# Reordering the start of a delta-rule and SwiGLU kernel: norms first, zero fills on another engine, two units alone in the first chain, filler products, and a written order that ends early

## The chip, the cores and the metric

The kernel runs on one core of one Trainium2 chip. The metric is the device time of a run in microseconds (us); the time before is the median of three runs. The profile is one execution of the same program, taken by the hardware profiler. Its engines are TensorE (PE; its weight loads are listed apart as PEld), VectorE (DVE), ScalarE (ACT), GpSimd (POOL) and SyncE (SP), which in the kernel before issues every DMA.

## The reference

Two blocks follow each other. The first is a delta-rule recurrence over 768 tokens, for 4 batches and 8 heads of width 48. Its output, seen as 3072 tokens of width 384, goes through an RMS norm and a SwiGLU feed-forward layer (FFN) of inner width 1536. All is float32; the four weight tensors are handed over as float64, and the kernel before reads them as pairs of 32-bit words and makes float32 of them on the chip.

```python
k_n = k / (np.linalg.norm(k, axis=-1, keepdims=True) + 1e-06)
for t in range(S):
    kt, vt, bt = (k_n[:, :, t], v[:, :, t], beta[:, :, t, None])
    y[:, :, t] = np.einsum('bhd,bhde->bhe', q[:, :, t], state)
    v_old = np.einsum('bhde,bhd->bhe', state, kt)
    state = state + bt[:, :, :, None] * np.einsum('bhd,bhe->bhde', kt, vt - v_old)
# ... x = y as (3072, 384)
xn = x / np.sqrt(np.mean(x * x, axis=-1, keepdims=True) + 1e-06) * rms_g
g = xn @ w_gate
out = (g * (1.0 / (1.0 + np.exp(-g))) * (xn @ w_val)) @ w_out
```

## The kernel before

Tokens are taken in chunks of 128, so there are 6 chunks of 4 units (one batch each). For each unit the keys are normalised, keys and queries are transposed (`kqt`), and their products (`gp`) are taken. Within a chunk the recurrence becomes a triangular system. Its 32x32 diagonal blocks, of all heads and batches at once, are gathered through DRAM (`gd`, `gblk`) and inverted by VectorE in 31 steps (`invert`). The inverses go back through DRAM (`td` to `tt`, and scaled `nd` to `ne`), and `recur` joins the blocks, solves, and updates the state. Every two units of output make one FFN group of 256 tokens.

Each part is a Python generator; `at(time, gen)` gives its place on a plan, and the plan's order is the written order of the program. Inside `manual_schedule` that order is kept on every engine. A plan unit is three FFN products and a little more: an FFN group takes 36.

```python
    def setup():
        # ... loads, constants, masks
        yield 3.5
        # ... beta transposed
        for t in [tt_all] + state:
            nc.gpsimd.memset(t, 0.0)
        nc.gpsimd.memset(gp_all[HC:C, :, 0:HC], 0.0)
        yield 6
        for n in range(B):
            load_v(n)
        load_k(B)

    def weights(times):                 # 18 pieces of 768 columns
        for (dst, src), raw, (time, dt) in zip(todo, raws, times):
            # ...
            nc.scalar.activation(out=top, in_=high.bitcast(FP32), func=ACTF.Copy, scale=2.0**-112)
            # ... five VectorE operations (L224 to L252), fetch() of a later piece before the last

    def normalize(n):
        kn = kpad[n % NK]
        nc.scalar.square(ksq, kn[:, :, 0:D])
        nc.vector.tensor_reduce(out=ksum, in_=ksq, axis=AXL.X, op=ALU.add)
        nc.vector.tensor_scalar_max(ksum, ksum, 1e-30)
        nc.gpsimd.tensor_tensor(out=knrm, in0=ksum, in1=half, op=ALU.pow)
        yield
        # ... + 1e-6, reciprocal, multiply

    def gather(n):                      # L337, L342
        for a in range(NBLK):
            nc.sync.dma_start(out=gds[c][...], in_=gp[b][...])
        if b == B - 1:
            nc.sync.dma_start(out=gblk, in_=gds.pop(c))

    def invert(c, dt):
        # ... ttb = identity
        for i in range(W - 1):          # 31 steps
            nc.vector.scalar_tensor_tensor(out=tmp, ...)        # L401
            nc.vector.tensor_tensor(out=to, in0=to, in1=tmp, op=ALU.add)   # L410
            yield dt
        nc.sync.dma_start(out=td, in_=ttb)
        nc.vector.tensor_tensor(out=gblk, in0=ttb..., in1=nbeta..., op=ALU.mult)
        nc.sync.dma_start(out=nd, in_=gblk)
        for b in range(B):
            # ... four tt loads from td (L426), two ne loads from nd (L431)

    def recur(c, dt):
        # corner: p_v, p_w -> vs, tt; inner: p_x, p_z -> x, u; outer: p_k, p_y, p_s -> v, y, state
        for s in range(-3, B + 2):
            inner(s, s - 1, s + 1)
            yield dt
            outer(s + 1, s - 1)
            yield dt
            corner(s + 3, s + 2)
            if s - 2 in units:
                transpose_y(B * c + s - 2, ys.pop(s - 2))
            yield dt

    def ffn(m, f0, f1):                 # FT = 12 feature blocks
        for f in range(f0, f1):
            # ... 6 products into p_gv (L645), sil on ScalarE (L654), h_f on VectorE (L656),
            # ... then the 2 products into p_o (L632) of the block before

    at(23, invert(0, 0.74))
    at(51.5, recur(0, 0.8))
    for i, m in enumerate((0, 1, 0, 1)):
        at(TF + CYC // 4 * i, ffn(m, half_f * (i // 2), half_f * (i // 2 + 1)))     # TF = 68, CYC = 72
    # ... weights: 3 pieces early, 5 from 47.5, 10 from TF + 1
    for c in range(1, NCH):
        t0 = TF - 16 + CYC * c
        for b in range(B):
            at(t0 - 57 + 5 * b, prepare(B * c + b))
        at(t0 - 30.5, invert(c, 0.55))
        at(t0 - 9, recur(c, 1.2))
        # ... two FFN groups at t0 + 16
    with tc.manual_schedule():
        run_plan()
```

Of the kernel before, what the change touches and what calls it, by code (L numbers as in the profile page):

```python
# [18 lines left out]
C = 128  # L19
# [8 lines left out]
def kernel(  # L28
# [74 lines left out]
    vraw = {}  # L103
# [30 lines left out]
    def setup():  # L134
# [25 lines left out]
        for i, p in enumerate((lo, hi)):  # L160
            nc.vector.tensor_tensor(
                out=mask[p, i], in0=row[p, p], in1=col[p, p], op=ALU.is_lt
            )
        yield 15
# [3 lines left out]
        yield 3.5  # L168
# [6 lines left out]
        for t in [tt_all] + state:  # L175
            nc.gpsimd.memset(t, 0.0)
        nc.gpsimd.memset(gp_all[HC:C, :, 0:HC], 0.0)
        yield 6
        for n in range(B):
            load_v(n)  # L180
        load_k(B)

# [28 lines left out]
    def weights(times):  # L211
        clock = 0
        for (dst, src), raw, (time, dt) in zip(todo, raws, times):
            yield time - clock
            clock = time + 5 * dt
            two = raw.bitcast(U32).rearrange("p (n two) -> p n two", two=2)
            low, high = two[:, :, 0], two[:, :, 1]
# [3 lines left out]
            top = bits.tile([128, WT], FP32, name="top", bufs=2)  # L221
            top_u, dst_u = top.bitcast(U32), dst.bitcast(U32)
            nc.scalar.activation(out=top, in_=high.bitcast(FP32), func=ACTF.Copy, scale=2.0**-112)
# [17 lines left out]
            yield dt  # L241

# [14 lines left out]
    def normalize(n):  # L257
# [4 lines left out]
        nc.vector.tensor_reduce(out=ksum, in_=ksq, axis=AXL.X, op=ALU.add)  # L262

        nc.vector.tensor_scalar_max(ksum, ksum, 1e-30)  # L264
        knrm = work.tile([128, H], FP32, name="knrm")
# [65 lines left out]
    def gather(n):  # L331
# [3 lines left out]
        for a in range(NBLK):  # L335
            o = diagonal(a)
            nc.sync.dma_start(  # L337
                out=gds[c][a * BH + b * H : a * BH + (b + 1) * H].rearrange("h r j -> r h j"),
                in_=gp[b][W * a : W * (a + 1), :, o : o + W],
            )  # L340
# [51 lines left out]
    def invert(c, dt):  # L392
# [3 lines left out]
        for i in range(W - 1):  # L396
# [13 lines left out]
            nc.vector.tensor_tensor(out=to, in0=to, in1=tmp, op=ALU.add)  # L410
            yield dt
        td = dram.tile([128, W, W], FP32, name="td")
# [9 lines left out]
        nc.sync.dma_start(out=nd, in_=gblk)  # L422
        for b in range(B):
            for a in (1, 3, 0, 2):
# [4 lines left out]
                )  # L429
            for a in (0, 2):  # L430
# [10 lines left out]
    def recur(c, dt):  # L441
# [35 lines left out]
        def outer(b_k, b_y):  # L477
# [11 lines left out]
            for h in range(H):  # L489
                for p, place in ((lo, Q0), (hi, Q1)):  # L490
# [7 lines left out]
                    )  # L498
            if c < NCH - 1:
# [10 lines left out]
                for par in range(2):  # L510
                    p = slice(DP * par, DP * (par + 1))
                    to = st[p, :, D * par : D * (par + 1)]
                    if c == 0:
                        nc.vector.tensor_copy(out=to, in_=p_s[p])
                    else:
                        nc.vector.tensor_tensor(out=to, in0=to, in1=p_s[p], op=ALU.add)
            if n + NK < NU:
                load_k(n + NK)
            if n + B < NU:
                load_v(n + B)  # L520
            ys[b_y] = norm(p_y)
# [59 lines left out]
        ys = {}  # L581
        for s in range(-3, B + 2):
# [4 lines left out]
            corner(s + 3, s + 2)  # L587
            if s - 2 in units:
# [3 lines left out]
    def norm(p_y):  # L592
# [10 lines left out]
        nc.vector.tensor_scalar_add(ms, ms, 1e-6)  # L603
        rs = work.tile([128, 1], FP32, name="rs")
        nc.gpsimd.tensor_tensor(out=rs, in0=ms, in1=mhalf, op=ALU.pow)  # L605
        nc.scalar.mul(y, p_y.rearrange("p h d -> p (h d)"), rs)
# [79 lines left out]
    def run_plan():  # L686
        heap = list(plan)
        heapq.heapify(heap)
        while heap:
# [9 lines left out]
    for n in range(B):  # L699

        times = (3.5 + 1.2 * n, 6.6 + 1.7 * n, 7.4 + 2.1 * n, 10.2 + 2.1 * n, 24 + 4 * n, 26 + 4 * n, 48 + 3 * n)
        at(0, prepare_first(n, [b - a for a, b in zip((0,) + times, times)]))
    at(23, invert(0, 0.74))
    at(51.5, recur(0, 0.8))
    half_f = FT // 2
    for i, m in enumerate((0, 1, 0, 1)):
# [4 lines left out]
            [(8.5 + 4.5 * i, 0.85) for i in range(3)]  # L711
            + [(47.5 + 4.2 * i, 0.8) for i in range(5)]
            + [(TF + 1 + 3.1 * i, 0.6) for i in range(10)]
        ),
    )
    for c in range(1, NCH):
        t0 = TF - 16 + CYC * c
        for b in range(B):
            at(t0 - 57 + 5 * b, prepare(B * c + b))
        at(t0 - 30.5, invert(c, 0.55))  # L720
        at(t0 - 9, recur(c, 1.2))
        for g in range(B // 2):
            at(t0 + 16 + CYC // 2 * g, ffn(B // 2 * c + g, 0, FT))
    with tc.manual_schedule():
        run_plan()
# [30 lines left out]
```

## Time and profile before

| what | before |
|---|---|
| time, median of 3 runs (lowest, highest) | 939.84 us (936.17, 942.12) |
| span of the profiled execution | 939.0 us |
| PE busy | 817.7 us (87%) |
| PEld busy | 628.8 us (67%) |
| DVE busy | 417.8 us (44%) |
| ACT busy | 247.4 us (26%) |
| POOL busy | 86.7 us (9%) |
| mean granted TensorE clock | 0.931 of full |

An engine's share is an average over stages that have different limits. The page also slices the run into 40 equal parts, with the busy share of each engine and the clock that TensorE was granted in tenths, and the trace can be asked for the busy time in any window and for what ended an engine's idle time. In the names, `out<-in` is what an instruction writes and reads, and L645 is line 645 of the kernel. A float32 product shows as two instructions in the trace. The first FFN product stands at 114.1 us, the four middle chunks take 140.7 to 142.1 us each, and the last stretch takes 100.6 us.

### The profile page before, as it was taken

The numbers are of one execution on the slowest core, as the hardware profiler recorded it, in microseconds if no ns is written. First come the engines' busy times: TensorE is split into PE (matmuls) and PEld (weight loads), VectorE is DVE, ScalarE is ACT, GpSimd is POOL, SyncE is SP. The second block draws the span as 40 slices with busy tenths as digits, with TensorE's granted clock in tenths as the row PEclk, the third lists the DMA queues.
The fourth block names the chain that finished last, engine by engine and source line by source line (L and its number), as shares of the span: only waits on it lengthen the run. The fifth ranks groups of instructions, "written<-read, shape, count | busy, mean of one in ns | idle before, by whom it ended". The sixth has DMA issues, their size and how long they took to land.

```text
span 939.0 us, 19558 instructions
## 1 busy us (share of the span) xinstructions
PE 817.7 (87%) x8270; PEld 628.8 (67%) x8270; DVE 417.8 (44%) x1053; ACT 247.4 (26%) x677; POOL 86.7 (9%) x94
## 2 busy tenths in 40 slices
PE   4516587879999979999979999979999979999998
PEld 3315465657777757777757777757777757777776
DVE  6796468893234292234283233283233283221010
ACT  4513234301314311324311324311324301221101
POOL 5000123000012100012100012100012100000000
PEclk8555689979999999999989999999999989999999
DMA  7724434303022103022203022203021103000000
GB/s 201 172 65 130 113 93 130 111 0 96 19 62 43 46 18 80 19 60 43 44 20 79 20 52 41 49 25 79 20 61 24 25 31 79 3 19 1 17 1 17
DMA packets 150935, 51.80 MB, mean 55 GB/s; under 512 B 142368, under 2 KB 145440, under 8 KB 150848
## 3 DMA queue, kind: packets, MB, share of 16 engines
q1 hardware_dynamic: 150848, 50.55, 22.0%
q8 instruction: 65, 1.06, 0.5%
q14 instruction: 22, 0.18, 0.1%
HBM read 36.37 MB, written 14.16 MB: 54 GB/s over the span
## 4 chain that ended last, share of the span: by engine, by line
PE 72%; DVE 12%; DMA 5%; ACT 5%; issue 3%; SPq 2%; POOL 1%; DVEq 0%; ACTq 0%; POOLq 0%
PE p_gv L645 36%; PE p_o L632 18%; DVE tmp L401 4%; DVE ttb L410 4%; PE p_y L491 3%; PE p_t L286 2%; PE p_g L302 2%; DMA gblk<-gd 2%; PE p_z L544 2%; PE p_k L526 2%; ACT gp L312 2%; ACT gp L311 2%; PE p_y L526 2%; DMA gd<-gp 1%; PE p_x L562 1%
## 5 line engine op out<-in xcount | busy, mean ns | idle before, releaser
L632 PE MATMUL p_o<-wo_sb,h_f 128*128 128x384 f32 x576 | 221.3, 509 | 42.3 <-DVE h_f L656 42.0
L645 PE MATMUL p_gv<-xt,wg_sb 128*128 128x256 f32 x864 | 222.3, 395 | 3.8 <-DVE xt L616 3.8
L645 PE MATMUL p_gv<-xt,wv_sb 128*128 128x256 f32 x864 | 215.3, 385 | 0.0
L645 PEld LDWEIGHTS p_gv<-xt,wg_sb 128*128 128x128 f32 x864 | 165.9, 197 | 48.5 <-DVE xt L616 4.2
L645 PEld LDWEIGHTS p_gv<-xt,wv_sb 128*128 128x128 f32 x864 | 162.8, 193 | 23.9 <-issue 1.4
L632 PEld LDWEIGHTS p_o<-wo_sb,h_f 128*128 128x128 f32 x576 | 106.0, 194 | 96.5 <-DVE h_f L656 51.3
L656 DVE TENSOR_TENSOR h_f<-sil,p_gv 128x256 f32<-128x256 f32 x144 | 60.2, 418 | 230.7 <-ACT sil L654 230.6
L654 ACT ACTIVATE sil<-p_gv 128x256 f32<-128x256 f32 x144 | 55.1, 383 | 241.4 <-PE p_gv L645 225.5
L401 DVE SCALAR_TENSOR_TENSOR tmp<-gblk,nbeta,ttb 128x31 f32<-128x31 f32 (+15 forms) x186 | 74.7, 402 | 33.3 <-DMA gblk<-gd 28.0
L605 POOL TENSOR_TENSOR rs<-ms,mhalf 128x1 f32<-128x1 f32 x24 | 15.0, 625 | 617.1 <-DVE ms L603 617.1
L410 DVE TENSOR_TENSOR ttb<-ttb,tmp 128x31 f32<-128x31 f32 (+15 forms) x186 | 63.7, 343 | 7.0 <-DVE tmp L401 0.3
L316 DVE TENSOR_TENSOR gp<-p_g,mask 64x128 f32<-64x128 f32 (+1 forms) x160 | 37.9, 278 | 51.6 <-ACT gp L312 47.0
L302 PE MATMUL p_g<-kqt 64*64 64x192 f32 (+2 forms) x896 | 46.3, 338 | 5.0 <-ACT kqt L291 4.0
L266 POOL TENSOR_TENSOR knrm<-ksum,half 128x8 f32<-128x8 f32 x24 | 40.6, 1696 | 105.7 <-DVE ksum L264 105.7
L291 ACT COPY kqt<-p_t 128x512 f32<-128x512 f32 x48 | 28.1, 586 | 70.1 <-PE p_t L286 69.8
L302 PEld LDWEIGHTS p_g<-kqt 64*64 64x64 f32 x896 | 34.8, 153 | 17.2 <-issue 8.4
L596 ACT ACTIVATE y<-p_y 128x384 f32<-128x384 f32 x24 | 11.8, 491 | 110.2 <-PE p_y L491 110.2
L562 PE MATMUL p_x<-tt,gp 64*64 64x64 f32 x384 | 30.7, 237 | 9.5 <-ACT tt L474 9.5
L311 ACT COPY gp<-p_g 128x128 f32<-128x128 f32 x96 | 25.6, 266 | 48.9 <-PE p_g L302 47.2
L472 ACT COPY vs<-p_v 32x256 f32<-32x256 f32 x48 | 17.4, 362 | 77.2 <-PE p_w L464 52.8
L457 PE MATMUL p_v<-tt,gp 32*32 32x32 f32 x768 | 19.6, 201 | 19.1 <-DMA tt<-td 19.1
L457 PEld LDWEIGHTS p_v<-tt,gp 32*32 32x32 f32 x768 | 16.7, 113 | 28.7 <-issue 26.5
(83 smaller groups left out, 757.6 us busy)
## 6 DMA issues: line engine op xcount, KB each, us to landing
kpad<-in_k_dram SPq DMA_DIRECT2D x24, 192.0 KB, 2.8
raw<-in_moe_w_gate_dram SPq DMA_DIRECT2D x6, 768.0 KB, 5.3
qpad<-in_q_dram SPq DMA_DIRECT2D x24, 192.0 KB, 3.3
raw<-in_moe_w_val_dram SPq DMA_DIRECT2D x6, 768.0 KB, 4.4
v_raw<-in_v_dram SPq DMA_DIRECT2D x24, 192.0 KB, 3.3
raw<-in_moe_w_out_dram SPq DMA_DIRECT2D x6, 768.0 KB, 4.6
out_dram<-o_sb SPq DMA_DIRECT2D x24, 192.0 KB, 1.9
gd<-gp SPq DMA_DIRECT2D x96, 32.0 KB, 1.7
```

Source lines behind the costliest of these rows:

```text
L266: nc.gpsimd.tensor_tensor(out=knrm, in0=ksum, in1=half, op=ALU.pow)
L302: nc.tensor.matmul(to, pair[d, K1 if i else K0], pair[d, places], skip_group_check=True)
L311: nc.scalar.copy(to[:, :, K0], p_g[:, :, K0])
L316: nc.vector.tensor_tensor(out=to[p, :, place], in0=p_g[p, :, place], in1=mask[p, i, None].to_broadcast([p.stop, 2, HC]), op=ALU.mult,)
L401: nc.vector.scalar_tensor_tensor(out=tmp, in0=gblk[:, i, None, i + 1 :].to_broadcast(shape), scalar=nbeta[:, c, i : i + 1], in1=ttb[:, 0 : ...
L410: nc.vector.tensor_tensor(out=to, in0=to, in1=tmp, op=ALU.add)
L526: nc.tensor.matmul(p_o[p, 2 * j : 2 * j + 2].rearrange("p h d -> p (h d)"), kq[:, j, place], st[:, j], start=(alone or j == 0), stop=alone ...
L562: nc.tensor.matmul(p_x[lo, h], gp[b_x][hi, h, HC * K0 : HC * (K0 + 1)], tt[b_x][hi, h], skip_group_check=True,)
L632: nc.tensor.matmul(p_o[i], h_f[:, i * C : (i + 1) * C], wo_sb[:, f], start=(f == f0), stop=(f == f1 - 1),)
L645: nc.tensor.matmul(p_gv[:, i], w_sb[:, t, f * 128 : (f + 1) * 128], xt[:, t], start=(t == 0), stop=(t == KT - 1),)
L654: nc.scalar.activation(out=sil, in_=p_gv[:, 0], func=ACTF.Silu)
L656: nc.vector.tensor_tensor(out=h_f, in0=sil, in1=p_gv[:, 1], op=ALU.mult)
```

## The change

The start is reordered, and some work goes to other engines.

- *Norms first.* All four units' norms stand ahead of the weight conversion on VectorE; the maximum goes to GpSimd, as does the addition in the RMS norm of the output. Two weight pieces instead of three come early, and each piece's first ScalarE step is written ahead, so that VectorE need not wait for it.
- *Zero fills* of `tt`, `gp` and the states go from GpSimd to ScalarE, spread between its copies.
- *Gathers* (`gd`) are issued by ScalarE, which wrote the data, and no longer by SyncE. `nd` is issued after the first unit's `tt` loads.
- *Two units alone.* In the first chunk, units 0 and 1 go through the recurrence by themselves, then units 2 and 3, so that the first FFN group can begin before units 2 and 3 are done. The state's update of the first chunk is a ScalarE copy, and it comes last.
- *Useless products.* TensorE multiplies the identity by itself, or by the inversion's intermediate, into a PSUM tile that nobody reads, to stay busy while it would wait.
- *Scale apart.* The norm's last multiplication is written a step after the norm, so that ScalarE does other work while GpSimd computes the factor.
- *Written order only up to half a cycle.* `manual_schedule` ends at plan time 104; what follows is ordered by the framework's own scheduler, and the plan's places for the later chunks are moved a little.

The diff, cut to its core:

```diff
+        p_fill.append(psum.tile([128, DM], FP32, name="p_fill", tag="out", bufs=2))
+        stay_warm(14)
...
-        for t in [tt_all] + state:
-            nc.gpsimd.memset(t, 0.0)
-        nc.gpsimd.memset(gp_all[HC:C, :, 0:HC], 0.0)
-        yield 6
+        yield 5
         for n in range(B):
             load_v(n)
         load_k(B)
+        yield 3
+        nc.scalar.memzero(tt_all)
+        yield 4
+        nc.scalar.memzero(gp_all[HC:C, :, 0:HC])
+        yield 4
+        for t in state:
+            nc.scalar.memzero(t)
+    def stay_warm(n, data=ident):
+        for i in range(n):
+            nc.tensor.matmul(
+                p_fill[0][:, 0 : data.shape[1]], ident, data, skip_group_check=True
+            )
...
-        nc.vector.tensor_scalar_max(ksum, ksum, 1e-30)
         knrm = work.tile([128, H], FP32, name="knrm")
+        nc.gpsimd.tensor_scalar_max(ksum, ksum, 1e-30)
...
-            nc.sync.dma_start(
+            nc.scalar.dma_start(
                 out=gds[c][a * BH + b * H : a * BH + (b + 1) * H].rearrange("h r j -> r h j"),
...
+            if c == 0 and i > W // 2:
+                stay_warm(2, tmp_b[:, 0 : min(128, n * (i + 1))])
             yield dt
+        if c == 0:
+            stay_warm(22)
...
-        nc.sync.dma_start(out=nd, in_=gblk)
         for b in range(B):
             # ... the four tt loads
+            if b == 0:
+                nc.sync.dma_start(out=nd, in_=gblk)
...
+            ys[b_y] = norm(p_y)
+            if c > 0:
+                update(b_y, u)
...
+        if c == 0:
+            for a, b in ((0, 1), (2, 3)):
+                corner(a, None)
+                stay_warm(warm)
+                yield dt
+                corner(b, a)
+                yield dt
+                # ... inner, corner, outer of a and b, with stay_warm(warm) between
+                transpose_y(a, scale(*ys.pop(a)))
+                stay_warm(warm)
+                yield dt
+                transpose_y(b, scale(*ys.pop(b)))
+                stay_warm(warm)
+                yield dt
+                update(a, u_a)
+                yield dt
+                update(b, u_b)
+                reload()
+                dt, warm = 1.2, 0
+                yield dt
+            return
...
-        nc.vector.tensor_scalar_add(ms, ms, 1e-6)
         rs = work.tile([128, 1], FP32, name="rs")
+        nc.gpsimd.tensor_scalar_add(ms, ms, 1e-6)
         nc.gpsimd.tensor_tensor(out=rs, in0=ms, in1=mhalf, op=ALU.pow)
+        return y, p_y, rs
+
+    def scale(y, p_y, rs):
         nc.scalar.mul(y, p_y.rearrange("p h d -> p (h d)"), rs)
...
-    at(23, invert(0, 0.74))
-    at(51.5, recur(0, 0.8))
+    at(20.9, invert(0, 0.74))
+    at(49, recur(0, 1.5, 3))
...
-            [(8.5 + 4.5 * i, 0.85) for i in range(3)]
-            + [(47.5 + 4.2 * i, 0.8) for i in range(5)]
-            + [(TF + 1 + 3.1 * i, 0.6) for i in range(10)]
+            [(12 + 4.2 * i, 0.8) for i in range(2)]
+            + [(46 + 4.2 * i, 0.8) for i in range(5)]
+            + [(TF + 1 + 3.1 * i, 0.6) for i in range(11)]
...
+        first = TF + 2 if c == 1 else t0 - 60
         for b in range(B):
-            at(t0 - 57 + 5 * b, prepare(B * c + b))
-        at(t0 - 30.5, invert(c, 0.55))
-        at(t0 - 9, recur(c, 1.2))
+            at(first + 4.5 * b, prepare(B * c + b))
+        at(first + 27, invert(c, 0.68))
+        at(*((t0 - 4, recur(c, 0.9)) if c == 1 else (t0 - 9, recur(c, 1.2))))
...
     with tc.manual_schedule():
-        run_plan()
+        run_plan(TF + CYC // 2)
+    run_plan()
```

In the program that results, each step's TensorE order is what the prediction counts from: after the change 120 FFN products stand ahead of the second chunk's recurrence, 102 before it; from the third chunk on both numbers are the same.

## The prediction

> **What bounds the kernel now.** I read four views: the page's slices for the course of the run, a table of windows cut at the kernel's own milestones, then the timeline in the two places where TensorE waits. A "unit" is one batch of one 128-token chunk; four units make a chunk, six chunks the run.
>
> From the page, busy tenths and granted clock in 40 slices of 23.5 us:
>
> ```profile
> PE   4516587879999979999979999979999979999998
> DVE  6796468893234292234283233283233283221010
> PEclk8555689979999999999989999999999989999999
> ```
>
> TensorE is full from the eighth slice on except one dent per chunk; the first five slices are half empty and at half clock; DVE is full just before each dent. The windows put numbers on it (start:end, length, then busy us of PE, weight loads, DVE, ACT, POOL, and the clock):
>
> ```profile
> 36.70:62.50 25.80, 6.20 (x72) 4.60 (x72) 23.09 (x62) 5.73 (x20) 0.00 (x0) 0.50 0.39 85
> 62.50:114.00 51.50, 26.57 (x646) 23.68 (x646) 33.50 (x54) 14.60 (x34) 3.44 (x4) 0.57 0.48 130
> 114.00:216.00 102.00, 83.75 (x477) 62.98 (x478) 81.90 (x182) 31.42 (x75) 14.49 (x11) 0.89 0.30 85
> 273.50:414.20 140.70, 131.89 (x1389) 100.95 (x1388) 58.32 (x164) 36.57 (x103) 12.93 (x15) 0.99 0.20 44
> 838.40:939.00 100.60, 97.15 (x455) 75.72 (x453) 11.76 (x28) 12.67 (x33) 0.54 (x1) 1.00 0.03 12
> ```
>
> First inversion (DVE alone), first recurrence (no engine full, clock 0.57), then from the first FFN product at 114 to the end of the second inversion at 216, where DVE converts weights, masks scores and inverts: 81.9 of 102. After that four chunks of about 141 us, TensorE-bound, and a tail. The dent in a chunk, from the timeline (start, length, engine, line, in brackets the idle time before and who ended it):
>
> ```profile
> 328.43 0.25 DVE L401 SCALAR_TENSOR_TENSOR tmp<-gblk,nbeta,ttb 128x31 f32<-128x31 f32 x1 [5.17 <-DMA gblk<-gd]
> 331.17 1.56 PE L632 MATMUL p_o<-wo_sb,h_f 128*128 128x384 f32 x4 [1.18 <-DVE h_f L656]
> 341.31 2.93 PE L632 MATMUL p_o<-wo_sb,h_f 128*128 128x384 f32 x4 [4.34 <-DVE h_f L656]
> ```
>
> DVE waits 5.17 for the gathered blocks with an h_f queued behind it, then runs 62 inversion operations with h_f spaced by up to 14 of them: TensorE loses 5.5 us, once per chunk. And the start:
>
> ```profile
> 11.76 3.27 DVE L224 TENSOR_SCALAR top<-top 128x768 uint32<-128x768 uint32 x1 [1.83 <-ACT top L223]
> 17.78 1.08 PE L286 MATMUL p_t<-ident,kpad 128*128 128x128 f32 x4 [4.78 <-DVE kpad L271]
> 84.61 0.89 ACT L223 ACTIVATE top<-raw 128x768 f32<-128x768 f32 x1 [4.31 <-DMA raw<-in_moe_w_out_dram]
> ```
>
> A weight operation that is 0.56 elsewhere takes 3.27 and delays unit 2's norm; at 84.6 ScalarE sits on a weight load for 4.31 with the recurrence's copies behind it.
>
> **What the Trainium skill says.** "SBUF — State Buffer", Who interferes with whom: a VectorE tensor_scalar in a two-port mode and GpSimd exclude each other for a whole instruction. The trace agrees: the 3.27 lies on GpSimd's zero fills (tt 1.80 from 11.38, state 1.50 from 13.12). "TensorE: Matmul & The Clock Gate", Part 1: idle default is half clock, full clock after some 3.4 us of sustained work. The trace agrees: six FFN instructions take 2.93 at 114 and 1.29 at 135. "DMA: Bandwidth & Descriptors", Anatomy of one DMA: a DMA's wait is spent on the issuing sequencer. So gd issued by ScalarE stops ScalarE; no run here shows that cost yet; on SyncE one issue takes 0.44.
>
> **The change, part by part.**
>
> 1. *Start of the first inversion.* With the fills gone from GpSimd and all norms ahead of the weights, unit 2's keys are ready at about 12 instead of 17.6. Then ScalarE limits: from 12.2 it has four units of eight copies (4 x 2.2), two transposed copies (1.2), two weight operations (1.8) and 16 gd issues. At SyncE's 0.44 these are 7 and the last ends at about 31, as now (29.9); at a quarter of it, near 26. I take the middle: inversion 1.5 us earlier.
>
> 2. *First recurrence.* Now: inversion end 62.5, first FFN product 114. After: tt of unit 0 lands as now (67.4). nd is issued only after unit 0's four tt (67.1 instead of 64.4), so ne and tt of unit 1 come some 2.8 later (73.1 against 70.3). Then units 0 and 1 alone: corner 1.3 + copies 1.5, p_x 2.0, p_z with p_x 3, p_z with p_u 2 + 0.8, p_y 2.0, at half-clock durations: p_y of unit 0 at about 86.5, of unit 1 at 89. The sixth weight piece, which the first FFN product needs too, is fetched behind all 24 tt and ne issues (about 82), lands at 87, and its shrink stands before the two norms on ScalarE. Norm, GpSimd's sum and power (1.5), scale, transpose, gain: second xt at about 92.5. Updates and the corners of units 2 and 3 (3 us) come before the first FFN product: 95.5, and with part 1 it is **94**, 20 earlier. The useless products cost nothing if the clock is up: one of 128 columns is half a 256-column FFN product (0.43 at full clock), 0.22; the 22 behind the inversion take 4.7, in the 4.9 until tt lands. At half clock they would take 9.5 and delay it by 4.6; 28 more ride on the last 14 inversion steps and should have raised the clock.
>
> 3. *From there to the second inversion's end.* Still DVE. In the new order 53 of the 90 weight operations follow the first h_f (53 x 0.72 = 38), with 32 masks (9), the inversion (25.8), 18 h_f (7.6), norms, u and xt (9), gblk (1.9): 91.5. The first h_f comes at about 99; at 90% use the end is at **201** instead of 216. The written order also lets 20 feature blocks of the FFN go before the second recurrence (120 products) instead of 17 (102): 3 x 3.88 = 11.6 more done. Together 26 us.
>
> 4. *Second recurrence.* Only 24 FFN products are left to lie between its steps, instead of 42. Each step's wait on ScalarE or DVE (1 to 2 us) shows on TensorE more often: minus 8. Net of 3 and 4: **18**.
>
> 5. *Chunks 2 to 5.* The scheduler leaves the recurrences at the same FFN products as before (246, 390, 534, 678), but the last scoring is nine products (5.8 us of TensorE) earlier, and two h_f instead of one stand between last mask and inversion. The 5.17 wait goes, and with h_f after 13, 9, 8, 11, 5, 11 operations DVE's worst lag behind TensorE falls: an inversion operation is 0.42 on average, 0.9 a pair in the middle, and TensorE needs 3.88 for a block. Now 12 and then 14 operations with their h_f take 5.9 and 6.8, together with the wait a lag near 5.5; then no stretch is longer than 5.4 and the others are about 4, a lag near 2. I take 3.5 per chunk: **14**. The short waits for PSUM in the scoring (2.1 per chunk) stay, and so does the tail.
>
> Sum: 940 - 18 - 14 = **908**. Cross-check by TensorE's work: 94 + FFN 144 blocks x 3.88 = 559 + units 2 and 3 of the first chunk 12 + five chunks of 38.7 = 193 + gaps (20 before and 8 in the second recurrence, 4 x 5.2 after) = 907. The 38.7 is a chunk's 141.2 less FFN 93.1 less gaps 9.4.
>
> **Rivals.** (a) *gd on ScalarE becomes a wait*: 16 issues a chunk, 7 us, in front of sil. For: ScalarE executes in order and must finish its own copies first. Against: it is 26% busy, and p_gv has two buffers. If half of a unit's 1.8 surfaces, 20 units cost 18: 926. (b) *The weights give the first gain back*: DVE is 80% busy from 114 to 216, so an earlier FFN only waits longer. If the second inversion's end gains only 5, the total is about 918. (c) *The scheduler's order gains nothing in the later chunks*: without part 5, 922. (d) *The clock stays up in the whole first chain*: products halve, FFN starts near 89, and with the DVE budget behind it about 4 more are gained: 904.
>
> **Range and chances.** The early stage is the surest, but (b) and (a) can each take ten or more; (d) and free gd issues give some 10. 893 to 926 should hold it 8 in 10. 2% is at 921. Faster 0.76, same 0.21, slower 0.03.
>
> **What would show it.** Part 1: first inversion operation near 35, no 3.27 on L224's successor. Part 2: first p_gv at 94; p_v of unit 1 about 2.8 later after the inversion than now. Part 3: gblk of the second chunk near 200, DVE at nine tenths before. Part 4: p_gv gone from between the steps there, TensorE waiting on ScalarE's copies. Part 5: chunks of 137 to 138, the waits for h_f below 2. Wrong if sil waits behind gd, if the useless products hold up p_v, or if the dent stays at 5.5.

## The result, and the profile after

| what | before | after |
|---|---|---|
| time, median (lowest, highest), 4 runs each side by side | 940.55 us (936.17, 942.12) | 883.07 us (882.07, 884.29) |
| ratio to before, 95% interval | 1 | 0.9396 [0.9362, 0.9431] |
| span of the profiled execution | 939.0 us | 881.3 us |
| TensorE (PE) busy | 817.7 us (87%) | 828.5 us (94%) |
| first FFN product | 114.1 us | 103.6 us |
| first `h_f` on VectorE | 128.3 us | 111.8 us |
| end of the second inversion (issue of its `td`) | 213.7 us | 210.4 us |
| second recurrence begins (its first `p_v`; the recurrence of the second chunk) | 221.6 us, behind 17 feature blocks | 216.7 us, behind 20 |
| sixth recurrence begins | 788.2 us | 731.9 us |

The prediction was 908 us with a range of 893 to 926. The kernel became faster, as said, but by 57 us where 32 were predicted.

The page of the changed kernel, busy tenths and granted clock in 40 slices of 22 us:

```profile
PE   6487798989999999999999999999999999999998
DVE  3786677886243393243392243492332491221110
PEclk8576799999999999999999999999999999999999
```

The dents of TensorE, one per chunk before, are gone from the tenth slice on, and so are the eights in the clock. The start is better filled, but still not full. The table of windows of the changed kernel (start:end, length, busy us of PE, weight loads, DVE, ACT, POOL, then the clock, the DMA share and GB/s):

```profile
35.30:62.50 27.20, 16.77 (x161) 13.72 (x159) 23.12 (x63) 10.51 (x35) 0.00 (x0) 0.64 0.38 85
62.50:111.80 49.30, 37.91 (x653) 34.02 (x652) 31.38 (x43) 15.81 (x36) 2.69 (x4) 0.76 0.49 135
111.80:210.40 98.60, 88.65 (x598) 66.07 (x596) 83.58 (x187) 35.46 (x87) 23.11 (x21) 0.97 0.34 91
0.00:210.40 210.40, 164.94 (x1621) 131.01 (x1622) 154.02 (x330) 82.04 (x210) 35.94 (x43) 0.84 0.43 113
390.60:521.90 131.30, 129.69 (x1389) 100.58 (x1388) 56.65 (x156) 37.91 (x104) 15.34 (x22) 1.00 0.21 47
521.90:652.50 130.60, 129.86 (x1390) 100.70 (x1389) 56.74 (x156) 37.93 (x105) 15.33 (x22) 1.00 0.21 48
781.50:881.30 99.80, 96.38 (x452) 75.17 (x450) 11.69 (x27) 12.27 (x31) 0.79 (x2) 1.00 0.03 12
```

Two things are to be seen. A middle chunk takes 131 us, not 141, and TensorE idles 0.7 to 1.6 us in it; before it idled 8.8 of 140.7. And up to the end of the second inversion VectorE works 154.0 us of 210.4, so it idles 56.4; before it worked 159.3 of 213.7 and idled 54.4. All the reordering at the start has not made VectorE less idle there.

What TensorE waited for in one middle chunk (waiting instruction, releaser: us in total, times, longest). The kernel before, 414.2 to 556.2:

```profile
PE p_o L632 <- DVE h_f L656: 6.3, 3, 3.0
PE p_t L286 <- ACT gp L312: 2.1, 3, 0.7
```

The changed kernel, 390.6 to 521.9:

```profile
PE p_o L719 <- DVE h_f L743: 1.6, 1, 1.6
```

And the place where VectorE had waited 5.17 us for the gathered blocks, in the changed kernel's timeline (start, length, engine, line, in brackets the idle time before):

```profile
306.69 0.42 DVE L743 TENSOR_TENSOR h_f<-sil,p_gv 128x256 f32<-128x256 f32 x1 [3.46 <-ACT sil L741]
307.03 0.24 DVE L428 SCALAR_TENSOR_TENSOR tmp<-gblk,nbeta,ttb 128x31 f32<-128x31 f32 x1
```

The inversion begins right behind an `h_f`, and the blocks are there already.

**Where the 57 us lie.** The two traces can be cut at the second and the sixth recurrence:

| stretch | before | after | gain |
|---|---|---|---|
| start to second recurrence | 221.6 | 216.7 | 4.9 |
| three feature blocks more done by then (3 x 3.88) | | | 11.6 |
| second to sixth recurrence | 566.6 | 515.2 | 51.4, less those 11.6: 39.8 |
| sixth recurrence to the last output's issue | 147.9 | 146.5 | 1.4 |
| sum | | | 57.7 |

The third line has a loss in it. Chunk by chunk its gain is 6.5, 10.6, 10.6 and 12.1 us. The first of these four, which holds the second recurrence, takes 122.8 us in the changed kernel, so with the three blocks 134.4, where a later chunk takes 130.5:

```profile
216.70:339.50 122.80, 121.93 (x1343) 95.48 (x1342) 56.27 (x155) 36.18 (x99) 15.33 (x22) 1.00 0.23 52
601.40:731.90 130.50, 129.76 (x1389) 100.64 (x1388) 55.83 (x152) 37.46 (x103) 11.48 (x17) 1.00 0.19 43
```

No wait of TensorE above 0.75 us stands in it; its small products (`p_v`, `p_w`, `p_x`, `p_y`, `p_z`, `p_xt`) follow each other more slowly, by some 4 us in all. That the few FFN products left between them are the reason fits part 4 of the prediction, but was not tested.

So parts 1 to 4 brought 16.5 of the first two lines less this 3.9: 12.6 (the prediction said 18). Part 5 brought 39.8 and 3.9: 43.7 (it said 14). The tail's 1.4 was in no part.

### The profile page after: what moved, and what is told of

It is laid out like the page before. It is cut to its first block, busy times and chain, and to the rows that moved or that the text cites. A ratio compares the mean times of both kernels' runs of the same rounds, so it can differ in the third digit from the quotient of the medians.

```text
span 881.3 us, 19880 instructions
## 1 busy us (share of the span) xinstructions
PE 828.5 (94%) x8434; PEld 646.7 (73%) x8434; DVE 404.7 (46%) x997; ACT 259.0 (29%) x691; POOL 97.7 (11%) x136
## 4 chain that ended last, share of the span: by engine, by line
PE 72%; DVE 9%; DMA 2%; ACT 2%; issue 1%; POOL 1%; ACTq 0%; SPq 0%
PE p_gv L732 36%; PE p_o L719 18%; DVE tmp L428 4%; DVE ttb L437 3%; PE p_g L329 3%; PE p_y L531 2%; PE p_t L313 2%; PE p_k L569 2%; PE p_z L587 2%; PE p_y L569 2%; PE p_x L605 1%; PE p_v L497 1%; PE p_z L596 1%; DMA gblk<-gd 1%; PE p_s L550 1%; DVE h_f L743 1%
## 5 line engine op out<-in xcount | busy, mean ns | idle before, releaser
L719 PE MATMUL p_o<-wo_sb,h_f 128*128 128x384 f32 x576 | 215.8, 497 | 11.1 <-DVE h_f L743 11.1
L732 PE MATMUL p_gv<-xt,wg_sb 128*128 128x256 f32 x864 | 217.3, 388 | 0.0
L732 PEld LDWEIGHTS p_gv<-xt,wg_sb 128*128 128x128 f32 x864 | 161.6, 193 | 39.4 <-issue 0.6
L719 PEld LDWEIGHTS p_o<-wo_sb,h_f 128*128 128x128 f32 x576 | 104.0, 190 | 62.7 <-DVE h_f L743 16.7
L293 POOL TENSOR_TENSOR knrm<-ksum,half 128x8 f32<-128x8 f32 x24 | 42.4, 1765 | 2.0
L688 POOL TENSOR_SCALAR ms<-ms 128x1 f32<-128x1 f32 x24 | 5.9, 247 | 328.0 <-ACT y L680 327.8
L420 POOL MEMSET ttb<- 128x1024 f32 x6 | 6.1, 1021 | 261.5 <-DMA td<-ttb 246.0
L587 PEld LDWEIGHTS p_z<-v_raw,tt 64*64 64x64 f32 x768 | 26.1, 142 | 8.8 <-issue 6.7
L531 PE MATMUL p_y<-u,gp 128*64 128x48 f32 x768 | 26.6, 222 | 3.4 <-DVE u L612 3.2
```

The source lines that it names most:

```text
L531: nc.tensor.matmul(p_y[p, h], gp[b_y][:, h, HC * place : HC * (place + 1)], u[:, h], start=(c == 0 and h == 0), stop=True, skip_group_chec ...
L587: nc.tensor.matmul(p_zs[b_z][p, h], tt[b_z][p, h], r[p, h], start=(h == 0), stop=(p is lo), skip_group_check=True,)
L719: nc.tensor.matmul(p_o[i], h_f[:, i * C : (i + 1) * C], wo_sb[:, f], start=(f == f0), stop=(f == f1 - 1),)
L732: nc.tensor.matmul(p_gv[:, i], w_sb[:, t, f * 128 : (f + 1) * 128], xt[:, t], start=(t == 0), stop=(t == KT - 1),)
```

## The experiments

Each kernel was timed against the kernel before on the same chip, and ratios are to that. "Places" are the plan times given with `at`; an "old" place is that of the kernel before.

### The places of the later chunks, put into the kernel before

The edit (`b_plan`): nothing but the third to sixth chunk's places, in written order to the end.

```diff
-            at(t0 - 57 + 5 * b, prepare(B * c + b))
-        at(t0 - 30.5, invert(c, 0.55))
+            at((t0 - 57 + 5 * b) if c == 1 else (t0 - 60 + 4.5 * b), prepare(B * c + b))
+        at(*((t0 - 30.5, invert(c, 0.55)) if c == 1 else (t0 - 33, invert(c, 0.68))))
```

> The kernel before with one thing of the change: from the third chunk on the keys' and queries' preparation stands at t0 - 60 + 4.5 b instead of t0 - 57 + 5 b, and the inversion at t0 - 33 with 0.68 between steps instead of t0 - 30.5 with 0.55. Everything stays in written order. Theory P (these places in the plan make the later chunks shorter): the four chunks fall from about 141 to about 131 us each, time about 900. Rival S (the scheduler that orders the later part makes the gain): 935 to 940. Rival W (moved work does it: gathers issued by ScalarE, scale written apart, additions on GpSimd): 935 to 940.

Measured: 904.19 us, ratio 0.9632 [0.9592, 0.9672]. One edit of numbers gives 34 of the 57 us. The inversions' ends lie 133.3, 132.3 and 132.3 us apart.

Of it, only the scoring's places (`b_prep`: the first of the two changed lines; the inversion stays at its old place with its old density):

> Half of the kernel above: only the preparation is moved (t0 - 60 + 4.5 b), the inversion keeps its place and its spacing of 0.55. If the loss in a chunk is mostly the wait for the gathered blocks and the waits for PSUM in the scoring, about 5 of the 10 us come off each chunk: about 920. If it is the density of the inversion on VectorE, it stays at 935 or above. Rivals S and W: 940.

Measured: 906.59 us, 0.966 [0.963, 0.9691], more than the 20 us expected. Nearly the whole gain of `b_plan` is here (the two intervals overlap; the inversions' ends lie 133.7 us apart against 132.3), so the inversion's denser or thinner spread mattered little. What went is the wait for the blocks. The timeline of VectorE with the scoring's places alone:

```profile
316.80 0.42 DVE L656 TENSOR_TENSOR h_f<-sil,p_gv 128x256 f32<-128x256 f32 x1 [3.46 <-ACT sil L654]
317.14 0.24 DVE L401 SCALAR_TENSOR_TENSOR tmp<-gblk,nbeta,ttb 128x31 f32<-128x31 f32 x1
```

The 5.17 ahead of L401 is gone, although the inversion is written where it was. TensorE's waits for PSUM in the scoring (`p_t` for `gp`) are gone too, which the prediction said would stay. All that is left of TensorE's waits from 395 to 527:

```profile
PE p_o L632 <- DVE h_f L656: 3.2, 2, 2.0
```

The second chunk's places as well (`b_plan1`, still the kernel before in all else):

```diff
+            at((TF + 2 if c == 1 else t0 - 60) + 4.5 * b, prepare(B * c + b))
+        at((TF + 2 if c == 1 else t0 - 60) + 27, invert(c, 0.68))
+        at(*((t0 - 4, recur(c, 0.9)) if c == 1 else (t0 - 9, recur(c, 1.2))))
```

> The kernel before with all places of the changed plan for later chunks, the second chunk's too (preparation from TF + 2, inversion 27 later at 0.68, recurrence at t0 - 4 and 0.9); written order, scale not apart. Theory L: the second chunk's places let more FFN products go before its recurrence while VectorE is full, worth 6 to 10 beyond the 904 of the later places: 894 to 898. If the second chunk gains only from the scheduler: 902 to 905.

Measured: 893.19 us, 0.9502 [0.947, 0.9534]. The second inversion ends at 210.9 and the second recurrence begins at 215.8 behind 18 blocks (222.0 behind 17 with the later places alone). So 45 of the 57 us are in the places, without the new start and without the scheduler.

### The scheduler

The changed kernel, with the old places from the third chunk on (`a_oldplan`):

```diff
-            at(first + 4.5 * b, prepare(B * c + b))
-        at(first + 27, invert(c, 0.68))
+            at((TF + 2 + 4.5 * b) if c == 1 else (t0 - 57 + 5 * b), prepare(B * c + b))
+        at(*((TF + 29, invert(c, 0.68)) if c == 1 else (t0 - 30.5, invert(c, 0.55))))
```

> The changed kernel with the places of preparation and inversion from the third chunk on put back to those of before (t0 - 57 + 5 b; t0 - 30.5, 0.55); the scheduler still orders this part. Theory P: the dents come back, about 920. Rival S: the scheduler mends the order, 883 to 888. Rival W: 883 to 888.

Measured: 894.13 us, 0.9529 [0.9501, 0.9557]. TensorE's waits in a chunk (395 to 527) of this kernel:

```profile
PE p_t L313 <- ACT gp L339: 2.0, 3, 0.7
PE p_v L497 <- DMA tt<-td: 0.3, 1, 0.3
```

With old places the scheduler removes every wait for `h_f`, and leaves those for PSUM. In written order the new places remove the waits for PSUM and more than half of those for `h_f`. They are two cures of largely the same ill, which is why their gains don't add.

The changed kernel in written order to the end (`a_written`):

```diff
-        run_plan(TF + CYC // 2)
-    run_plan()
+        run_plan()
```

> The changed kernel with the written order kept to the end: no scheduler at all. Theory P: 880 to 887, since the order from the third chunk on is the same on TensorE either way; only the second chunk's recurrence differs, a few us at most. Rival S: 905 to 920. Rival W: 880 to 887.

Measured: 890.53 us, 0.9488 [0.9449, 0.9528], 7.5 more than the changed kernel's 883.07 (8.6 by the ratios). Its timeline of TensorE around the second inversion:

```profile
186.96 2.93 PE L719 MATMUL p_o<-wo_sb,h_f 128*128 128x384 f32 x4 [5.31 <-DVE h_f L743]
...
214.58 0.21 PE L497 MATMUL p_v<-tt,gp 32*32 32x32 f32 x2 [1.85 <-DMA tt<-td]
```

An `h_f` written behind inversion steps costs 5.31 here, and the second recurrence stands behind 18 blocks, not 20, and waits for its data.

The places and the scheduler in the kernel before, and nothing else of the change (`b_plan1s`: the two edits above together):

> The kernel before with all the changed places, and ordered by the framework's scheduler from plan time 104 on; nothing else of the change. Theory S (what is missing between the places alone, 893, and the best form, 877, is the scheduler): about 880, the chunks near 130.5 instead of 132.5, first h_f as in the places alone (124.6), end of the second inversion 205. Rival R (8 of the 16 us come from the first recurrence's small moves, which bring the first h_f from 124.6 to 117.1 and the second inversion's end from 210.9 to 203.1): chunks near 130.5, but the second inversion still ends near 210, and the whole is 885 to 886.

Measured: 881.38 us, 0.9395 [0.9364, 0.9426]. The changed kernel's ratio is 0.9396. TensorE's waits in one chunk in written order (`b_plan1`, 395.4 to 527.9):

```profile
PE p_o L632 <- DVE h_f L656: 2.7, 2, 1.4
```

and with the scheduler (`b_plan1s`, 387.9 to 518.5):

```profile
PE p_o L632 <- DVE h_f L656: 0.7, 1, 0.7
```

The inversions' ends move from 132.5 to 130.5 us apart. Between the third and the sixth recurrence this makes 6.1 of the scheduler's 10 us; 1.4 more lie behind the sixth, and 2.4 between the first inversion's end and the third recurrence. There 236 FFN instructions of the first kind (`p_gv`) stand ahead of the second recurrence, not 216, which is 1.7 blocks or 6.5 us of TensorE's work, but only 2.4 of it are left at the third.

### The new start, taken apart

Since places and scheduler alone give the whole gain, the rest of the change must sum to nothing, within the intervals. Single parts were taken out of the changed kernel. Four units together in the first recurrence, with the useless products of the start and of the inversion kept (`a_four`):

```diff
-        if c == 0:
+        if False:
...
-    at(49, recur(0, 1.5, 3))
+    at(49, recur(0, 0.8))
```

> The changed kernel with the first chunk's recurrence as before: all four units together (steps of 0.8 on the plan), no useless products in it; everything else stays, with the 14 and 50 useless products at the start and around the inversion. Theory E (two units alone bring the first FFN product forward, and this is worth most of the early gain): first FFN product at 112 to 114 instead of 103.6, time 893 to 897. Rival D (VectorE sets the end of the second inversion whatever the start): 883 to 887.

No useless products at all (`a_nofill`: `for i in range(0)` in `stay_warm`):

> The changed kernel without any useless product. Theory H (they only lie in the chain, since the clock falls to half between them anyway): first FFN product at 98 to 100 instead of 103.6, time 879 to 882. Rival C (they hold the clock up and that carries the first chain): first FFN product at 106 or later, 886 to 892.

None in the first recurrence only (`a_nochain`: `recur(0, 1.5, 0)`):

> The changed kernel with the useless products kept at the start and around the inversion, and left out only in the first recurrence (six groups of three). Theory H: these groups stand 1.5 us each in the chain at half clock; first FFN product at 97 to 99, time 878 to 881. Rival C: 884 to 890.

`nd` issued ahead of the `tt` loads again (`a_ndfirst`):

> The changed kernel with nd issued ahead of the first unit's tt loads, as before. If the order of these issues delays unit 1 as worked out (p_v of unit 1 at 72.9, 10.4 after the inversion, before it 7.8), p_v of unit 1 comes 2.5 earlier, first FFN product near 101, time 881 to 883. If another chain (weights, ScalarE) sets the first FFN product: no change, 883 to 884.

The scale right after the norm again (`a_noscale`):

> The changed kernel with the norm's last multiplication written right after the norm again. In the kernel before ScalarE stood 1.5 us on GpSimd's power with a sil behind it, and TensorE lost 1.2 us once a chunk at the end of an FFN group. If that is the cause of the 1.2: they come back, 888 to 891, with one more stop of TensorE per chunk. If the scheduler moves sil ahead by itself: 883 to 885.

| run | us | ratio [95%] | first FFN product | second inversion's end |
|---|---|---|---|---|
| changed kernel | 883.07 | 0.9396 [0.9362, 0.9431] | 103.6 | 210.4 |
| `a_four` | 879.34 | 0.9377 [0.9354, 0.9399] | 112.1 | 208.2 |
| `a_nofill` | 880.16 | 0.9388 [0.937, 0.9407] | 101.2 | 208.5 |
| `a_nochain` | 880.87 | 0.9399 [0.938, 0.9417] | 102.8 | 210.0 |
| `a_ndfirst` | 879.99 | 0.9392 [0.9368, 0.9416] | 100.3 | 206.6 |
| `a_noscale` | 881.01 | 0.9385 [0.9355, 0.9415] | 102.4 | 206.9 |

None of the five differs from the changed kernel by more than the intervals. `a_four` tells most: two units alone bring the first FFN product 8.5 us earlier (103.6 against 112.1), and the second inversion ends no earlier for it. `a_ndfirst` shows the price of the later `nd`: unit 1's first `p_v` comes 7.9 us after the inversion, not 10.4, and the first FFN product at 100.3, and the whole is no faster for that either.

How the useless products delay the first recurrence is to be seen in the changed kernel's timeline of TensorE, of which these are the rows with useless products or with a wait:

```profile
94.59 0.90 PE L702 MATMUL p_xt<-ident,y 128*128 128x128 f32 x3 [1.95 <-ACT y L693]
95.29 1.49 PE L194 MATMUL p_fill<-ident 128*128 128x128 f32 x6
...
97.20 1.49 PE L194 MATMUL p_fill<-ident 128*128 128x128 f32 x6
...
102.20 0.21 PE L504 MATMUL p_w<-vs,ne 32*32 32x32 f32 x1 [1.58 <-ACT vs L512]
```

Three of them (six instructions) take 1.49 us. The clock did rise with them: from the inversion's end to the first FFN product it is 0.74, in `a_nofill` 0.50. What they win in clock they take in time: the first FFN product comes at 101.2 without them and at 103.6 with them. Counted from the end of the first inversion, which is 62.5 to 64.3 in these profiles, it comes after 41.1 us with them, after 38.5 in `a_nochain` and after 38.6 in `a_nofill`. So it is the 18 products within the first recurrence that cost 2.5 us there, and the 22 behind the inversion that cost nothing. The inversion is 27.2 us long with them and 26.1 in `a_nofill`.

The whole start put back (`a_lateonly`): four units, no useless products, zero fills on GpSimd, `nd` first, three early weight pieces, and the first chunk's old places. Kept are the later places, the scheduler, the gathers on ScalarE, the first weight step written ahead, the additions on GpSimd, the first state's copy on ScalarE and the scale apart.

```diff
-        nc.scalar.memzero(tt_all)   # ... and gp_all, state
+        for t in [tt_all] + state:
+            nc.gpsimd.memset(t, 0.0)
...
-    at(20.9, invert(0, 0.74))
-    at(49, recur(0, 1.5, 3))
+    at(23, invert(0, 0.74))
+    at(51.5, recur(0, 0.8))
```

> The changed kernel with its start put back: four units together in the first recurrence, no useless products, zero fills on GpSimd, three weight pieces early and the old places for the first chunk's steps, nd ahead of tt. Kept are the places and the scheduler of the later chunks, the scale apart, gd on ScalarE, the weight pieces' first step written ahead. Theory L (all of the gain is in what happens after the first FFN product): 878 to 885. Rival E (the new start has its share): 888 or above.

Measured: 877.1 us, 0.9339 [0.9308, 0.937]. Its windows:

```profile
63.60:117.10 53.50, 30.46 (x737) 26.67 (x737) 33.77 (x48) 19.40 (x47) 3.27 (x8) 0.68 0.52 139
117.10:203.10 86.00, 78.34 (x423) 57.33 (x423) 77.06 (x176) 30.58 (x75) 20.33 (x17) 0.98 0.31 86
0.00:203.10 203.10, 134.13 (x1454) 102.89 (x1454) 157.44 (x329) 76.81 (x204) 38.74 (x49) 0.82 0.45 117
```

This fits an account of why the new start is worth nothing. The first `h_f` comes at 117.1, later than the changed kernel's 111.8, and yet the second inversion ends 7.3 us earlier. VectorE has 157.4 us of work up to that end and idles 45.7; in the changed kernel it has 154.0 and idles 56.4. The start of the change brings the FFN forward by leaving weight work for later (two early pieces and not three), and VectorE is emptier for it: by 5.0 us before the first inversion, and by 6.1 us between the first `h_f` and the second inversion's end. In every kernel with two early pieces VectorE idles 18.5 to 20.8 us ahead of the first inversion, in every one with three 11.0 to 16.7. The number of early pieces was not changed by itself, so that this is the cause is argued and not shown.

Could a freer VectorE end the second inversion earlier? The last addition of the late weight pieces on GpSimd (`c_pool`: four units, no useless products, `nd` first, and this):

```diff
-            nc.vector.tensor_tensor(out=dst, in0=dst, in1=top, op=ALU.add)
+            (nc.gpsimd if i >= 7 else nc.vector).tensor_tensor(out=dst, in0=dst, in1=top, op=ALU.add)
```

> A version meant to be faster: four units together, no useless products, nd ahead of tt, and the last addition of the eleven late weight pieces on GpSimd, which takes 11 x 0.95 off VectorE where VectorE sets the pace. Theory D (VectorE's sum sets the end of the second inversion): that end comes 6 to 9 earlier, time 872 to 876. Rival: the addition is slow on GpSimd or stops VectorE while it reads, 880 to 890.

Measured: 885.91 us, 0.9435 [0.9403, 0.9467], and the end came at 212.6, later. In its timelines of GpSimd and VectorE:

```profile
114.62 2.34 POOL L292 TENSOR_TENSOR knrm<-ksum,half 128x8 f32<-128x8 f32 x1
116.94 1.81 POOL L278 TENSOR_TENSOR wo_sb<-wo_sb,top 128x768 f32<-128x768 f32 x1
119.14 0.83 POOL L297 TENSOR_TENSOR kpad<-kpad,krec 128x384 f32<-128x384 f32 x1 [0.40 <-issue]
117.00 1.78 DVE L295 TENSOR_SCALAR knrm<-knrm 128x8 f32<-128x8 f32 x1 [1.57 <-POOL knrm L292]
```

The addition takes 1.81 there and 0.96 on VectorE, and stands between the norm's power and its last product. It also holds VectorE up: VectorE's operation on `knrm`, 0.17 elsewhere, takes 1.78 and ends with the addition (118.78 and 118.75), and the ten first operations of the weight pieces (`top` from `top`) between the first `h_f` and the second inversion's end take 12.6 us, where `a_four` has 6.4. VectorE is busy 84.9 us in that stretch, 80.5 in `a_four`. It was not made freer, so the question stays unanswered. The Trainium skill, "GPSIMD Engine Reference", 3.1 Elementwise — side-by-side cycle accounting, states 1.96 times VectorE's time for such an addition of 2048 elements; the 1.9 measured here at 768 agrees.

### What is useful in the rest

Three parts that `a_lateonly` keeps were taken out of it, one each. The first recurrence's small moves (`l_rs`):

```diff
-                        nc.scalar.copy(to, p_s[p])
+                        nc.vector.tensor_copy(out=to, in_=p_s[p])
...
-        nc.gpsimd.tensor_scalar_add(ms, ms, 1e-6)
+        nc.vector.tensor_scalar_add(ms, ms, 1e-6)
...
+        nc.scalar.mul(y, p_y.rearrange("p h d -> p (h d)"), rs)     # in norm, and no longer in scale
```

> The best form so far (start put back, places and scheduler kept, 877), with the first recurrence's small moves put back: the RMS norm's addition on VectorE, its scale right after the norm, and the first state written by VectorE. Theory R: first h_f some 5 to 7 later than 117.1, the second inversion's end near 209, the whole 883 to 885. Theory S: no change, 877.

Measured: 881.98 us, 0.9401 [0.9376, 0.9426], against 0.9339 [0.9308, 0.937]. The first `h_f` comes at 120.9 (117.1), the second inversion ends at 208.6 (203.1). Where the time goes shows the timeline of TensorE from the first FFN product on. In `l_rs`:

```profile
108.78 1.75 PE L727 MATMUL p_gv<-xt,wg_sb 128*128 128x256 f32 x6 [2.20 <-DVE xt L698]
110.46 1.94 PE L591 MATMUL p_z<-u,x 64*64 64x48 f32 x16
112.33 2.93 PE L727 MATMUL p_gv<-xt,wv_sb 128*128 128x256 f32 x6
```

and in `a_lateonly`:

```profile
107.94 1.56 PE L727 MATMUL p_gv<-xt,wg_sb 128*128 128x256 f32 x6 [0.65 <-DVE xt L698]
109.44 1.13 PE L591 MATMUL p_z<-u,x 64*64 64x48 f32 x16
110.49 1.56 PE L727 MATMUL p_gv<-xt,wv_sb 128*128 128x256 f32 x6
```

In `l_rs` the first state's copies (0.71) and a weight operation (0.96) stand ahead of `xt` in VectorE's queue (from 106.43 to 108.17), TensorE waits 2.20 for it and not 0.65, and behind that wait the granted clock is half for 6.8 us: the same products take 2.93 and not 1.56. The waits of ScalarE for the norm's factor differ little, 0.9 in `l_rs` and up to 0.5 in `a_lateonly`. This is the one part outside places and scheduler that is worth something, 5 to 6 us.

The first weight step inside its piece again (`l_noshrink`):

```diff
-            top = tops[i]
+            top = shrink(raw)
```

> The best form so far (877), with each weight piece's first ScalarE step written inside its piece again instead of one piece ahead. If writing it ahead is what brought the first h_f to 117: VectorE waits about 1 to 2 us for ScalarE in each of the 10 pieces between first h_f and second inversion, so that its busy time before the second inversion falls from 98% to near 85% and the end comes 5 to 10 later, 884. If VectorE finds other work in the gap: 877 to 879.

Measured: 874.77 us, 0.9321 [0.9289, 0.9353]. Writing it ahead gains nothing: the second inversion ends at 202.0 without it, and at 203.1 with it.

The gathers on SyncE again (`l_gdsync`: `nc.sync.dma_start` for `gd`):

> The best form so far (877), with the gathers issued by SyncE again. If their issue on ScalarE (0.45 each, 16 a chunk) delays sil or copies, this is faster by up to 4; if they are free there, and SyncE's queue is free for the loads and stores, slower by 1 to 3. My own view: within 2 of 877.

Measured: 875.19 us, 0.933 [0.9304, 0.9355], the same within the intervals.

Last, the version made of what is useful, places, scheduler and the small moves (`l_best`: `a_lateonly` with the two last edits), beside the changed kernel on the same chip (`after_again`):

> The changed kernel without its new start, without the shrink written ahead and with the gathers on SyncE; kept are the places, the scheduler and the first recurrence's small moves (additions on GpSimd, scale apart, first state written by ScalarE). If the two single steps (874.8 and 875.2 from 877) add: 873, ratio 0.930. If their gains were only the scatter of when the first inversion starts: 876, 0.933.

> The changed kernel itself once more, on the same chip as the version made of its useful parts, so that the two can be set side by side: 883 (0.940). If the useful parts alone are better, their interval lies below this one's: 0.930 to 0.933 against 0.940. If the new start is worth nothing either way, the two differ by less than 3 us.

Measured: 876.48 us, 0.9338 [0.9302, 0.9374], against 881.85 us, 0.9395 [0.9371, 0.9419]. The four versions without the new start lie at 0.9321 to 0.9339, the changed kernel at 0.9395 and 0.9396. In this pair the intervals overlap by 0.0003; taken with the others, the new start costs some 5 us and wins none. `l_best` is no better than `l_noshrink` or `l_gdsync` alone: those two edits don't add.

The whole account, in ratios: later chunks' places 0.9632, second chunk's 0.9502, scheduler 0.9395, small moves to about 0.934, new start back to 0.9396.

## Why the prediction was wrong

**The step that failed is part 5, by its size.** "I take 3.5 per chunk: 14" should have been nearly 11: 43.7 over the four chunks, of which the slower second recurrence took back 3.9. The mechanism was named rightly (the wait of 5.17 for the blocks goes, `h_f` no longer lags). The sizes were off in four places:

- "A lag near 2" was left over for TensorE. The waits for `h_f` in a middle chunk fell from 6.3 to 1.6 us, or 0.7.
- "The short waits for PSUM in the scoring (2.1 per chunk) stay" is wrong: `b_prep` shows them gone with the scoring's places alone, `a_oldplan` shows them staying without.
- A further wait for `h_f` of 1.15 us, once in each chunk before (at 411.6, 553.6 and 694.7), outside the dent, was not in the count. It goes too: with the places alone (`b_plan1`) it still takes 1.22, with the scheduler it is gone.
- The clock was left out. After each dent the products ran slowly for a while: in the dent that the prediction shows, four `p_o` instructions take 2.93 behind the wait of 4.34 and 1.56 behind one of 1.18. The same 1,390 instructions are busy 132.1 us in a chunk before (556.2 to 697.3) and 129.9 after: 2.3 more. The Trainium skill, "TensorE: Matmul & The Clock Gate", Why this matters for your kernels, says that gaps above some 3 us bring the clock back to half. The trace agrees for 4.34 and 1.18, but not on the limit: in the chunk before, gaps of 2.16 and 3.01 (at 473 and 483) were each followed by 3.4 us of half clock, and the same products are busy 133.6 there. The prediction cites that page for the start and does not use it for the dents.

Idle 8.96 to 0.74 and busy 132.1 to 129.9: together 10.5, the whole difference of that chunk.

**Part 1** is right in what it counts and wrong in what it brings. The inversion begins at 35.3 (predicted near 35), the operation of 3.27 is gone, and `gd` takes ScalarE 1.8 us for four, as at SyncE. That the start is met is luck: the last `gd` is issued by 30.7, no earlier than before (29.9), and landed 1.2 us later where it had been 3.0, which the prediction did not count; and the start scatters by some 4 us anyway (last section). But the inversion is 27.2 us long and not 25.8, because of the useless products riding on it, and ends at 62.5 as before.

**Part 2** fails: 103.6 and not 94. `p_v` of unit 1 comes 10.4 us after the inversion, 7.8 before, 2.6 later where 2.8 were worked out. The useless products were held to cost nothing "if the clock is up"; it was up only in part (0.74), and those in the chain cost 2.5. For the other 7 us there are waits in the chain that the sum of durations left out, such as 1.95 for `y` and 1.58 for `vs` above; they were not followed one by one.

**Part 3.** The second inversion's end is 210.4, not 201. VectorE is 85% busy from the first `h_f` on, not 90%, and begins 13 us later than assumed. The three blocks more are right: 11.6.

**Part 4.** The loss came by half, and not in the form predicted: from 187 to 319 us the changed kernel's TensorE has no wait above half a microsecond, but the small products of the second recurrence's stretch are slower by some 4 us (3.9 of the predicted 8).

So parts 1 to 4 make 12.6 where 18 were predicted, and even that comes of errors that cancel in part: 15 for the earlier second inversion was really 5, and 8 of loss was really 3.9.

Two readings of the slices are off by little, and nothing rests on them: TensorE is full from the tenth slice on, not the eighth, and VectorE is full in the slice of each dent, not just before it.

**The rivals.** (b), the weights give the first gain back, is what happened: 16.5 us gained at the first `h_f`, 3.3 left at the second inversion's end. (a) did not happen: ScalarE stands 0.45 us for each `gd`, and with `gd` back on SyncE the time is the same (875.2 against 877.1). (c) is the opposite of what happened: the later chunks brought most of the gain, by the places first and the scheduler on top. (d) did not come about (clock 0.74).

What stays open: why VectorE idles 15 us between first `h_f` and second inversion in the changed kernel and 9 in `a_lateonly` was not followed to single waits. How much of the small moves' 5 us is the addition, the scale or the copy was not separated; the scale by itself made no difference in the changed kernel, and the half clock behind the longer wait was seen in one profile of `l_rs` only.

## What to carry to other kernels

When a dent recurs in every stage of a long kernel, price the whole of it: all waits in it, and the slower products behind it. An edit of two numbers in each stage was worth more here than the whole rebuilt start. Before an early stage is shortened, ask which engine sets its end and how long that engine idles up to there: if its idle time doesn't shrink, an earlier first product is given back. Filler work on TensorE did raise the clock here (0.50 to 0.74), but each filler takes its turn in the same queue: those within the chain of the first recurrence cost 2.5 us, and none of them made the kernel faster.

## What the runs showed of the hardware that was not expected

- The price of a dent is its wait and then the clock: 2.3 us on top of 8.2 of idle time in the chunk from 556 to 697, and 3.9 in the one before it, where the gaps were shorter (2.16 and 3.01).
- Behind a gap of 1.85 to 3.42 us the clock fell to half in some cases and not in others. The same gap of 2.72 near 186 us was followed by half clock in one profile of the changed kernel and not in the other (`after_again`). Behind each of the fifteen gaps of 3.64 us and more, from 120 us on in all runs, it was half.
- While GpSimd adds two 768-wide float32 tiles (1.81 us), an operation of VectorE that takes 0.17 elsewhere stood for 1.78 (`c_pool`).
- Useless products raised the mean clock of the first recurrence from 0.50 to 0.74 and did not shorten it.
- Four DMA issues hold ScalarE 1.8 us, no more than SyncE (1.8 to 1.9); the first chunk's gathers land 1.2 us after ScalarE's last issue, and 2.4 to 3.2 after SyncE's; moving 16 a chunk either way changed nothing (875.2 against 877.1).
- The first inversion begins at 32.6 in one kernel's profile and at 36.6 in another's (`b_prep`, `b_plan`) although their programs are the same up to there. Single profiles of the start are therefore read to some 4 us only, and small steps need the medians.
